# Linear attention feeding a sparse mixture of attention experts, on one core: key tails projected and multiplied once per two head pairs, part of the key sums by accumulating transfers, and the order of the steps as a list

## Chip, cores and metric

The kernel runs on one core of a Trainium2 chip. The metric is the device time of one execution in microseconds, 617.24 us as the median of three runs before the change (616.54 to 617.45).

## What is computed

The reference has two stages, each with B = 8 batches and S = 576 positions.

The first is linear attention over H = 8 heads of 64 columns. For q and k of every head a feature map phi projects 64 columns to 128, subtracts the largest absolute value of the row and takes exp of the result and of its negative, so that phi has 256 columns:

```python
proj = x @ w_phi; proj -= max(abs(proj), axis=-1)
phi = concatenate([exp(proj), exp(-proj)])
kv = phi(k).T @ v;  z = sum over positions of phi(k)
x = (phi(q) @ kv) / (phi(q) @ z + 1e-6)
```

The second takes x as [B, S, 512] and has E = 4 experts of causal softmax attention with a head of 64 columns each (projections wq, wk, wv, wo, scores scaled by 1/8). A gate of 4 logits per position picks the best two experts, and the output is their weighted sum.

## The kernel before

**Tiling.** Heads are taken in 32 pairs p (4 pairs for each batch b). 576 positions are 4 blocks of 128 and a tail of 64. The projections of phi, the products with v, z and the attention run in fp32; the three projections of x, the scores and the output projection run on a split of each operand into a high and a low part (hi, lo), as three matmuls hi x hi, hi x lo, lo x hi.

**Stages of a pair.** `load_k`, `load_q` and `load_v` bring the inputs on SP's queue. `stream_k` (L511) projects k: eight matmuls of 64 rows x 128 columns (`half_mm`, L506 to L509), one for each head and block, two of them side by side on the upper and lower 64 rows of the array, and a ninth for the tails of both heads. `center` (L558) takes the row maxima (L564) and subtracts them into `ek` (L578) on VectorE. ScalarE takes exp twice (act, L326, 1152 columns each). `key_sum` (L542) then adds the four blocks of phi(k) into `zs` by three VectorE additions (L546), for the pairs from p = 4 on. `stream_kv` (L589) multiplies: L605 has v's 32 columns as the weights and phi(k) as the moving operand, 4 blocks and a tail for each of two heads and two halves of v, 20 matmuls of 256 columns. L622 gives z: from p = 4 on with `zs` against ones and the tails against `sel`, 8 matmuls of 128 columns; before p = 4 with all five pieces, 20 matmuls. The result is turned (L641 or L633) and, from p = 6 on, sent through DRAM (`kvd`) into `kv`.

`stream_q` (L652) projects q, `phi_q` (L676) takes its maxima with GpSimd's PARTITION_ALL_REDUCE (L681), subtracts (L685) and takes exp. `stream_n` (L692) makes denominators (L710) and numerators (L721); `fractions` (L726) turns the denominators by VectorE (L732), adds eps by ScalarE into the PSUM bank, takes the reciprocal there (L739) and spreads it (L745); `divide` (L749) makes x in its hi and lo parts.

**Stages of a batch.** `stream_b` (L768) projects x to queries and keys (`proj_t`, L315 through the helper `mm`), makes scores (L838), copies them out (L324), masks them on GpSimd (L942). `maxima` (L945) finds the column maxima (L955, and PARTITION_ALL_REDUCE at L959), subtracts (L963) and starts the exps. `proj_v` (L859) projects x to values and gate logits: for each of 5 position blocks 12 matmuls of 260 columns, the fifth with 64 positions only. `sums` (L986, L1001), `attend` (L1010, L1030), `evac_y`, `out_unit` and `store` finish the batch.

**PSUM.** All products go through one pool of 8 banks of 512 columns, tag `c`. A bank is taken when a step is placed and given back at `plan.release`.

**Order.** Every engine works in the order in which the program's planner wrote the instructions (`in_order` fixes it). The planner is a list scheduler that runs while the program is built: each stream yields a `Step` with its engine and what it needs; `Plan.loop` picks, among the steps that could start within 53 ns of the earliest, the one with the lowest position (`MOVE`, `POS1`, `POS`, `BOFF`), with an allowance for a change of TensorE's tiling. Steps that copy out of PSUM choose between ScalarE and VectorE by cost. TensorE's tilings here are 128 x 128 (L315, L633), 64 rows x 128 columns (L509, L838) and 128 rows x 32 columns (L605, L622, L710, L721, L924, L1001, L1030).

```python
for t in range(NJ):
    for h in range(2):
        u_ = 4 * h + t if t < 4 else 8
        for k in range(2):
            g = slice(64 * k + 32 * h, 64 * k + 32 * h + 32)
            nc.tensor.matmul(o[g, 0:2], v_in[:, 4 * h + t if t < 4 else 8 + h, k:64:2], ...)
```

Of the kernel before, what the change touches and what calls it, by code (L numbers as in the profile page):

```python
# [26 lines left out]
KC = 640  # L27
# [9 lines left out]
CACT = ()  # L37
TAILPE = True
RB = 2
PXB = 5  # L40
HOT = 22.62
SLOPE = (-27.1, -45.11, 31.37, 22.04, 0.2)
UB = 4
SADD = 2
LAST = 7
KADD = 3
KPOOL = 0
FLEX = (544, -30)
QB = 1
PSUB = 0  # L50
# [4 lines left out]
WINDOW = 53.0  # L55
SWITCH = 43.0
SLACK = 150.0
LATE = (1200.0, 500.0)
PHASE = 0.0
ZEROS = 34.47  # L60

MOVE = {
# [32 lines left out]
NPAIRS = B * NP  # L95
HEAD = 2.29
ADDS = (0, 2)
KVD = 6
RATE = 2.18
TRATE = 2.37  # L100
CHANGE = (150.0, 190.0)
PORT = 350.0
OTHER = 20.47
LDW = 109.0
PSUM_TILES = (("c", 8, 512),)


def moved(x, i):
# [1048 lines left out]
```

## Time and profile before

| what | value |
|---|---|
| median of three runs | 617.24 us (616.54 to 617.45) |
| span of the profiled execution, first to last instruction | 615.0 us |
| time of the profiled execution by itself | not given apart from its span |
| instructions | 19992 |
| TensorE (PE) busy | 600.5 us, 98% |
| weight loads (PEld) busy | 470.6 us, 77% |
| VectorE (DVE) busy | 557.3 us, 91% |
| ScalarE (ACT) busy | 432.0 us, 70% |
| GpSimd (POOL) busy | 245.0 us, 40% |
| mean granted TensorE clock | 0.997 |
| moved by DMA | 52.48 MB |

A busy time is the union of an engine's instructions. Matmuls overlap: the next starts while the one before drains, so what a matmul costs the engine is the distance between starts, or the length of a piece of the chain of waits, and not its own duration. The chain of waits goes back from the last instruction to what released each one. A piece of it gives start, length, what ran and how often.

### The profile page before, as it was taken

What the parts mean: (1) busy time and instruction counts of PE and PEld (TensorE: products, weight loads), DVE (VectorE), ACT (ScalarE), POOL (GpSimd) and SP (SyncE); (2) the same over time, 40 slices, a digit from 0 to 9 for tenths busy, and PEclk for the clock granted to TensorE, in tenths of its full rate; (3) what the DMA queues carried; (4) which work ended last, traced back from release to release, by engine and by line L of the source; (5) the groups of instructions that cost most, each with busy time, mean ns of one, the idle gap of its engine ahead of it and who ended that gap; (6) DMA issues with size and microseconds to landing.
All of it is one profiled execution on the core that took longest, in us unless ns stands there. A gap on an engine that the chain in (4) does not pass through costs nothing.

```text
span 615.0 us, 19992 instructions
## 1 busy us (share of the span) xinstructions
PE 600.5 (98%) x8263; PEld 470.6 (77%) x8263; DVE 557.3 (91%) x1124; ACT 432.0 (70%) x1034; POOL 245.0 (40%) x167
## 2 busy tenths in 40 slices
PE   8999999999999999999999999999999999999987
PEld 7665788667796778768886868876889677878976
DVE  5899989999999999999899999999999998888793
ACT  4898786667687688677775885875796668556652
POOL 5635533453324644252333614418430706421420
PEclk9999999999999999999999999999999999999999
DMA  9553212253113431253214332144212311020022
GB/s 218 155 150 103 59 51 81 68 159 87 54 66 113 120 87 37 72 158 110 74 35 107 119 107 63 46 135 138 66 53 83 111 37 27 15 92 2 2 78 78
DMA packets 41610, 52.48 MB, mean 85 GB/s; under 512 B 21168, under 2 KB 24624, under 8 KB 41520
## 3 DMA queue, kind: packets, MB, share of 16 engines
q1 hardware_dynamic: 41200, 50.62, 28.5%
q8 instruction: 65, 1.06, 0.7%
q10 hardware_dynamic: 320, 0.59, 0.4%
q14 instruction: 25, 0.20, 0.1%
HBM read 36.64 MB, written 14.55 MB: 83 GB/s over the span
## 4 chain that ended last, share of the span: by engine, by line
PE 74%; DVE 15%; ACT 5%; DMA 2%; issue 2%; POOLq 1%; POOL 1%; SPq 0%; ACTq 0%; DVEq 0%
PE ps_c L315 29%; PE ps_c L509 9%; PE ps_c L605 9%; PE ps_c L721 7%; PE ps_c L1030 6%; PE ps_c L838 6%; PE ps_c L710 4%; DVE u L685 3%; DVE zs L546 2%; PE ps_c L622 2%; ACT ek L326 2%; PE ps_c L1001 1%; DVE s L963 1%; DVE ek L578 1%; DVE max L975 1%
## 5 line engine op out<-in xcount | busy, mean ns | idle before, releaser
L681 POOL PARTITION_ALL_REDUCE mx<-u x64 | 144.2, 2305 | 182.7 <-ACT u L324 165.9
L315 PE MATMUL ps_c<-xh,qk 128*128 128x320 f32 (+1 forms) x512 | 106.1, 298 | 0.0
L959 POOL PARTITION_ALL_REDUCE max<-top x16 | 59.9, 3745 | 101.5 <-DVE top L955 35.8
L315 PEld LDWEIGHTS ps_c<-xh,qk 128*128 128x128 f32 x512 | 82.7, 188 | 2.3 <-issue 0.7
L326 ACT ACTIVATE ek<-ek 128x1152 f32<-128x1152 f32 x64 | 75.0, 1171 | 5.7 <-DVE ek L578 5.0
L315 PE MATMUL ps_c<-xl,qk 128*128 128x256 f32 (+1 forms) x256 | 75.5, 295 | 0.0
L605 PE MATMUL ps_c<-ek,v_in 128*32 128x256 f32 x1280 | 75.4, 381 | 0.0
L963 DVE TENSOR_TENSOR s<-s,max 128x1152 f32<-128x1152 f32 (+4 forms) x80 | 68.3, 879 | 1.0 <-POOL max L959 1.0
L942 POOL TENSOR_SCALAR_AFFINE_SELECT s<-s 128x256 f32<-128x256 f32 (+1 forms) x80 | 41.5, 558 | 62.2 <-ACT s L324 61.9
L685 DVE TENSOR_TENSOR u<-u,mx 128x576 f32<-128x576 f32 x64 | 61.6, 975 | 3.9 <-POOL mx L681 3.9
L324 ACT COPY s<-ps_c 128x512 f32<-128x512 f32 (+4 forms) x152 | 52.7, 445 | 14.7 <-PE ps_c L838 14.4
L326 ACT ACTIVATE s<-s 128x1152 f32<-128x1152 f32 (+4 forms) x80 | 56.4, 740 | 8.6 <-DVE s L963 8.4
L605 PEld LDWEIGHTS ps_c<-ek,v_in 128*32 128x32 f32 x1280 | 39.7, 110 | 27.2 <-issue 1.3
L315 PE MATMUL ps_c<-vg,xh 128*128 128x260 f32 (+1 forms) x320 | 58.9, 286 | 0.3 <-ACT s L324 0.3
L564 DVE TENSOR_REDUCE pmax<-ps_c 128x4 f32<-128x512 f32 (+1 forms) x96 | 49.5, 539 | 8.1 <-PE ps_c L509 8.0
L315 PE MATMUL ps_c<-yh,wo 128*128 128x320 f32 (+1 forms) x256 | 53.1, 303 | 0.0
L326 ACT ACTIVATE mx<-u 128x576 f32<-128x576 f32 x64 | 43.9, 687 | 10.5 <-DVE u L685 10.4
L324 ACT COPY u<-ps_c 128x256 f32<-128x256 f32 (+1 forms) x127 | 41.6, 412 | 11.7 <-PE ps_c L509 11.4
L578 DVE TENSOR_TENSOR ek<-ps_c,pmax 128x512 f32<-128x512 f32 (+1 forms) x96 | 49.8, 537 | 0.0
L315 PEld LDWEIGHTS ps_c<-vg,xh 128*128 128x128 f32 (+1 forms) x320 | 47.4, 177 | 1.9 <-ACT s L324 0.8
L509 PEld LDWEIGHTS ps_c<-wf,k_in 64*128 64x128 f32 x576 | 41.9, 190 | 8.5 <-ACT u L324 3.0
L509 PE MATMUL ps_c<-wf,k_in 64*128 64x128 f32 x576 | 46.7, 283 | 1.5 <-ACT u L324 1.1
(124 smaller groups left out, 1399.4 us busy)
## 6 DMA issues: line engine op xcount, KB each, us to landing
v_in<-in_v_dram SPq DMA_DIRECT2D x32, 320.0 KB, 3.0
out_dram<-ot SPq DMA_DIRECT2D x32, 288.0 KB, 2.1
q_in<-in_qt_dram SPq DMA_DIRECT2D x60, 144.0 KB, 2.9
kvd<-kvt SPq DMA_DIRECT2D x104, 48.0 KB, 1.7
kv<-kvd SPq DMA_DIRECT2D x26, 192.0 KB, 2.6
k_in<-in_kt_dram SPq DMA_DIRECT2D x32, 144.0 KB, 2.8
k_in<-in_kt_dram SPq DMA_DIRECT2D x32, 128.0 KB, 2.8
q_in<-in_qt_dram ACTq DMA_DIRECT2D x4, 144.0 KB, 4.1
```

Source lines behind the costliest of these rows:

```text
L315: nc.tensor.matmul(o, a, b, start=start, stop=stop, skip_group_check=True)
L324: nc.scalar.copy(o, i)
L326: nc.scalar.activation(o, i, func, **kw)
L509: nc.tensor.matmul(o, a, b, start=True, stop=True, skip_group_check=True)
L564: dve(n * 128, [mk], [pk]).tensor_reduce(out=m[:, us], in_=src, axis=AX.X, op=ALU.max, apply_absolute_value=True)
L578: dve(n * 128, [e1k], [pk, mk]).tensor_tensor(out=ek2[p % EKB][:, 1, us, :], in0=src, in1=m[:, us].unsqueeze(2).to_broadcast([128, n, 128] ...
L605: nc.tensor.matmul(o[g, 0:2], v_in[:, 4 * h + t if t < 4 else 8 + h, k:64:2], ek[:, :, u_, :].rearrange("p c (w f) -> p c w f", w=4), star ...
L681: nc.gpsimd.partition_all_reduce(M, U, 128, bass_isa.ReduceOp.absmax)
L685: (nc.gpsimd if st.eng == 'POOL' else nc.vector).tensor_tensor(out=U, in0=U, in1=M, op=ALU.subtract)
L721: nc.tensor.matmul(ps[g:g + 32, 0:n], kvi[:, 2 * k + h, 32 * c:32 * c + 32], P_[h][c][:, s0:s1], start=c == 0, stop=c == 1, skip_group_che ...
L959: nc.gpsimd.partition_all_reduce(big.rearrange("p e s -> p (e s)"), top.rearrange("p e s -> p (e s)"), 128, bass_isa.ReduceOp.max)
L963: dve(2 * (S - 128 * j), [('d', x, j)], [('max', z)], 1.11, True).tensor_tensor(out=block(s_, j, None, rows(j)), in0=block(s_, j, None, ro ...
```

## The change

The parts of the diff, one by one. The first is the order: positions, costs and allowances of the planner go, and `Plan.loop` reads a list of 3100 characters, each the number of the stream that moves next. A second list of 520 digits says which engine makes each copy (0 ScalarE, 1 VectorE); 93 of the digits are 1. In the kernel before, VectorE made 32 such copies.

```diff
+    def loop(self):
+        sides = iter(SIDES)
+        for c in ORDER:
+            s = self.streams[ord(c) - 48]
...
+            if isinstance(st.eng, tuple):
+                st.eng = st.eng[int(next(sides))]
```

Key tails of four heads (two pairs) are loaded, projected, centred and put through exp together, as `kt_in`, `ekt`; k's main part keeps four blocks (`KC` 512, `ek` of 8 blocks, so exps of 1024 columns):

```diff
+    def load_tails():
+        for m in range(NT):
+            yield Step('SP', pred=has('proj_t', m - 1) if m else None)
+            src = kt[2 * m:2 * m + 2, :, 512:896].rearrange("q d (h t) -> (q d) h t", h=2)[:, :, 0:64]
+            load(kt_in.rearrange("p (h t) -> p h t", h=2), src, 'kt_in')
...
+    def stream_tails():
+        for m in range(NT):
+            banks = yield Step('PE', 'c', ready, n=2)
+            for a, (pk, ps) in enumerate(banks):
+                r = slice(64 * a, 64 * a + 64)
+                half_mm(ps[:, 0:128], kt_in[r, :], wf[r, 0:128], 128, pk, need)
...
+            act(256, ekt[:, 0], ekt[:, 1], ['et0'], ['et1'], AF.Exp)
+            yield Step('ACT')
+            act(256, ekt[:, 1], ekt[:, 1], ['et1'], [], AF.Exp, scale=-1.0)
```

Their products with v and with ones come first into the two PSUM banks of the two pairs, in a tiling of 64 rows x 32 columns, and the blocks are added to them. Both banks are taken before the first pair's products:

```diff
+    def tail_products(banks):
+        for h in range(2):
+            r = slice(64 * h, 64 * h + 64)
+            for k in range(2):
+                for a, (pk, ps) in enumerate(banks):
+                    g = 64 * k + 32 * (h ^ a)
+                    nc.tensor.matmul(three(ps)[g:g + 32, 0:2], vt_in[r, a, h, k:64:2], ekt[r, :, a].rearrange(...),
+                                     start=True, stop=False, skip_group_check=True)
...
+            if p % 2 == 0:
+                banks = yield Step('PE', 'c', lambda: ('phi_t', p // 2) in done and ('load_vt', p // 2) in done, n=2)
+                tail_products(banks)
+            odd, (kc, ps) = p % 2, banks[p % 2]
-            for t in range(NJ):
+            for t in range(4):
...
-            for t in range(first + TAILPE if adds else NJ):
+            for t in range(1 if adds else 4):
```

The sum of the blocks of phi(k): blocks 0 and 1 are written to `zs` by ScalarE as exps of their own (two of 512 columns), blocks 2 and 3 are added to them by one transfer with accumulation from GpSimd's queue, and VectorE adds the two halves:

```diff
+        if adds:
+            yield Step('ACT', pred=has('kv', p - 1))
+            for c in range(2):
+                act(512, zs[:, c].rearrange("p a h f -> p (a h) f"), ek[:, 1, 0:4], ['zs'], [e1k], AF.Exp, scale=1.0 - 2.0 * c)
...
+    def key_sum(p, ek, ekk):
+        yield Step('POOL')
+        add_to(zs.rearrange("p c a h f -> p c (a h f)"), ek[:, :, 4:8, :].rearrange("p c u f -> p c (u f)"), 'zs', ekk)
+        yield Step('DVE')
+        dve(512, ['zs'], [], 1.11, True).tensor_tensor(out=zs[:, :, 0], in0=zs[:, :, 0], in1=zs[:, :, 1], op=ALU.add)
...
+    def add_to(o, i, w, r):
+        nc.gpsimd.dma_start(o, i, accum_op=ALU.add)
```

The factors of `fractions` lie in SBUF (`facs`, two buffers for each of its two uses), so the PSUM bank goes back after the first turn:

```diff
-        both = ps[:, S // 2:S // 2 + 18]
+        both, fk = facs[a][n % 2], f'fac{a}{n % 2}'
         dve(S // 2, [key], [pk], 1.15).transpose(X[:, 0:S // 2], ps[:, 0:S // 2])
+        plan.release('c', (pk, ps))
...
-        plan.release('c', (pk, ps))
```

In `proj_v` the fifth block takes the last 64 positions of x's hi and lo parts side by side as 128 weight columns (`x_end`, copied by ScalarE after `divide`), 8 matmuls where there were 12; the lower half of the result is copied out by ScalarE and the upper half added to it by VectorE:

```diff
+        if s1 == S:
+            yield Step('ACT')
+            act(128, x_end[i], xT2[i][:, :, S - 64:S], [f'xe{i}'], [f'xh{i}', f'xl{i}'])
...
+                    for x_, w_ in ((0, 0), (0, 1), (1, 0)) if m == 128 else ((None, 0), (None, 1)):
...
+                act(260, vs[:m, j], ps[m:128, 0:260], [f'vs{j}', 'lg'], [kc])
+                yield Step('DVE')
+                dve(260, [f'vs{j}', 'lg'], [kc]).tensor_tensor(out=vs[:m, j], in0=ps[:m, 0:260], in1=vs[:m, j], op=ALU.add)
```

The loads follow: k in two transfers a pair for three, v with 8 blocks for 10, and for every two pairs one transfer of key tails and one of v's tails.

## Rows read from the trace of the kernel before

**Rows 1.** Page, busy time by engine, and the chain of waits by engine.

```profile
PE 600.5 (98%) x8263; PEld 470.6 (77%) x8263; DVE 557.3 (91%) x1124; ACT 432.0 (70%) x1034; POOL 245.0 (40%) x167
PE 74%; DVE 15%; ACT 5%; DMA 2%; issue 2%; POOLq 1%; POOL 1%; SPq 0%; ACTq 0%; DVEq 0%
```

**Rows 2.** Busy time by stretch: stretch, length, PE, PEld, DVE, ACT, POOL (instructions), clock, DMA.

```profile
0.00:25.00 25.00, 22.85 (x299) 18.46 (x299) 16.93 (x47) 15.25 (x29) 13.01 (x13) 1.00 0.78 199
...
250.00:275.00 25.00, 25.00 (x400) 17.06 (x400) 23.49 (x54) 16.10 (x46) 12.61 (x5) 1.00 0.44 131
...
575.00:600.00 25.00, 22.37 (x304) 20.21 (x300) 22.10 (x42) 16.95 (x43) 8.32 (x7) 0.98 0.13 49
600.00:615.00 15.00, 11.06 (x124) 9.21 (x116) 4.56 (x10) 3.78 (x12) 0.00 (x0) 0.92 0.21 80
```

**Rows 3.** Chain of waits in order of time: start, length, work (xcount).

```profile
14.40 1.31 PE ps_c L509 x18
...
257.34 1.09 PE ps_c L509 x16
...
260.73 0.44 PE ps_c L622 x16
...
268.84 2.30 PE ps_c L605 x40
...
293.27 2.16 PE ps_c L605 x40
...
298.62 0.89 PE ps_c L509 x16
```

**Rows 4.** Timeline of PE, the fifth block of the value projection: start, length, work.

```profile
584.41 0.40 PE L315 MATMUL ps_c<-vg,xh 128*64 128x260 f32 x2
...
585.85 0.40 PE L315 MATMUL ps_c<-yh,wo 128*128 128x256 f32 x2
```

**Rows 5.** Groups by line and form, PE's warm-up matmuls.

```profile
L315 PE MATMUL ps_c<-warm 128*128 128x128 bf16 x117 | 8.8, 241 | 1.0 <-DVE col L356 1.0
```

**Rows 6.** Groups by line and form, VectorE: busy us, mean ns.

```profile
L546 DVE TENSOR_TENSOR zs<-zs,ek 128x512 f32<-128x512 f32 x56 | 42.4, 757 | 0.5
L546 DVE TENSOR_TENSOR zs<-ek 128x512 f32<-128x512 f32 x28 | 21.6, 772 | 0.6 <-ACT ek L326 0.4 <-PE ps_c L622 0.2
L1044 DVE TENSOR_TENSOR ps_c<-ps_c,rb 128x256 f32<-128x256 f32 x16 | 6.7, 418 | 0.4 <-PE ps_c L1030 0.2
```

**Rows 7.** Groups by line and form, ScalarE: busy us, mean ns.

```profile
L326 ACT ACTIVATE ek<-ek 128x1152 f32<-128x1152 f32 x64 | 75.0, 1171 | 5.7 <-DVE ek L578 5.0
L326 ACT ACTIVATE s<-s 128x640 f32<-128x640 f32 x16 | 11.8, 739 | 0.8 <-DVE s L963 0.8
L326 ACT ACTIVATE s<-s 128x384 f32<-128x384 f32 x16 | 8.4, 526 | 0.0
L326 ACT ACTIVATE s<-s 64x128 f32<-64x128 f32 x16 | 4.8, 302 | 0.3 <-DVE s L963 0.3
L324 ACT COPY u<-ps_c 128x256 f32<-128x256 f32 x64 | 20.7, 377 | 10.8 <-PE ps_c L509 10.5
```

**Rows 8.** The tile of key sums: count, shortest/median/longest ns, first and last start.

```profile
L622 PE MATMUL ps_c<-zs,ones x224: 272/273/298, 53.9 to 522.5; 128*32 128x128 f32 x112
```

**Rows 9.** DMA issues: queue, count, KB each, us to landing.

```profile
v_in<-in_v_dram SPq DMA_DIRECT2D x32, 320.0 KB, 3.0
...
kvd<-kvt SPq DMA_DIRECT2D x104, 48.0 KB, 1.7
kv<-kvd SPq DMA_DIRECT2D x26, 192.0 KB, 2.6
```

**Rows 10.** Timeline, VectorE beside GpSimd, at the start of the kernel.

```profile
8.10 8.50 POOL L681 PARTITION_ALL_REDUCE mx<-u  x4 [6.79 <-ACT u L324]
...
11.53 0.74 DVE L685 TENSOR_TENSOR u<-u,mx 128x576 f32<-128x576 f32 x1
...
12.40 1.86 DVE L685 TENSOR_TENSOR u<-u,mx 128x576 f32<-128x576 f32 x1
```

**Rows 11.** Waits of PE: waiter, what ended it, us in total, times, longest.

```profile
PE ps_c L1001 <- DVE max L975: 2.6, 1, 2.6
...
PE ps_c L509 <- ACT u L324: 1.1, 2, 0.6
```

More of the change, by code (lines that the diff above doesn't have):

```diff
@@ L181, in run @@
             cost = self.clocked(t, cost, rows)
-        if port:
+        if eng == 'DVE' and port:
             cost += self.blocked(t)
+            self.shared = (t, t + cost)
+        if eng == 'POOL' and self.shared[0] < t < self.shared[1]:
+            t = self.shared[1]
         end = t + cost
@@ L186, in run @@
         if eng == 'POOL':
-            self.pool = [*self.pool[-7:], (t, end)]
+            self.pool = [*self.pool[-7:], (t, t + port)]
         for k in r:
@@ L231, in release @@
         self.psum[tag].append(t)
-    def start(self, st):
-        best = None
-        for eng, cost in st.eng if isinstance(st.eng, tuple) else ((st.eng, 0.0),):
-            t = self.free.get(eng, 0.0)
-            for k in st.needs:
-                t = max(t, self.after(self.ready, k, eng) + st.slack)
-            if st.tag is not None:
-                t = max(t, sorted(self.after(self.last, k, eng) for k, _ in self.psum[st.tag])[st.n - 1])
-            if eng == 'DVE' and st.port:
-                cost += self.blocked(t)
-            if best is None or t + cost < best[0]:
-                best = t + cost, t, eng
-        return best[1:]
@@ L273, in loop @@
                 self.streams.remove(s)
+        assert not self.streams
 def in_order(tc):
@@ new lines, in stream_k, with phi_k @@
+            done.add(('proj_k', p))
+            plan.spawn(phi_k(p))
+    def phi_k(p):
+        i = p % EKB
+        ek, e0k, e1k = ek2[i], f'ek{i}0', f'ek{i}1'
+        adds = ADDS[p >= NP]
+        yield Step('ACT', pred=lambda: all((('center', p, t) in done for t in range(2))))
+        act(1024, ek[:, 0], ek[:, 1], [e0k], [e1k], AF.Exp)
+        if adds:
[3 more added lines that the diff above has]
+        yield Step('ACT')
+        act(1024, ek[:, 1], ek[:, 1], [e1k], [], AF.Exp, scale=-1.0)
+        if adds:
+            plan.spawn(key_sum(p, ek, [e0k, e1k]))
+        done.add(('phi_k', p))
@@ new lines, in stream_tails @@
+    def stream_tails():
+        for m in range(NT):
+            need = ['kt_in', 'wphi']
+            ready = lambda: ('load_t', m) in done and ('w', 0) in done and (not m or ('kvt', m - 1) in done)
+            banks = yield Step('PE', 'c', ready, n=2)
+            for a, (pk, ps) in enumerate(banks):
+                r = slice(64 * a, 64 * a + 64)
+                half_mm(ps[:, 0:128], kt_in[r, :], wf[r, 0:128], 128, pk, need)
+            done.add(('proj_t', m))
+            for a, (pk, ps) in enumerate(banks):
+                plan.spawn(center_tail(m, a, pk, ps))
+            yield Step('ACT', pred=lambda: all((('center_t', m, a) in done for a in range(2))))
+            act(256, ekt[:, 0], ekt[:, 1], ['et0'], ['et1'], AF.Exp)
+            yield Step('ACT')
+            act(256, ekt[:, 1], ekt[:, 1], ['et1'], [], AF.Exp, scale=-1.0)
+            done.add(('phi_t', m))
@@ L559, in center @@
         m, mk = pmax[p % 2], ('pmax', p % 2, t)
-        us = slice(4 * t, min(9, 4 * t + 4))
-        n = us.stop - us.start
-        src = ps[:, 0:n * 128].rearrange("p (u f) -> p u f", f=128)
-        yield Step('DVE', [pk], hot=True)
-        dve(n * 128, [mk], [pk]).tensor_reduce(out=m[:, us], in_=src, axis=AX.X, op=ALU.max,
-                                               apply_absolute_value=True)
-        free = has('kv', p - EKB) if p >= EKB else None
-        e0k, e1k = f'ek{p % EKB}0', f'ek{p % EKB}1'
@@ L568, in center @@
[L568 to L579 removed]
+        us = slice(4 * t, 4 * t + 4)
@@ L589, in stream_kv, with three @@
+    def three(ps):
+        return ps[:, 0:384].rearrange("p (w c f) -> p c w f", w=4, c=3)
     def stream_kv():
+        banks = None
         for p in range(NPAIRS):
@@ L895, in gates @@
         G = 'gate'
-        yield Step('DVE', ['lg'], pred=lambda: all(('v', b, j) in done for j in range(NJ)) and (not b or ('gate', b - 1) in done))
+        yield Step('DVE', pred=lambda: all((('v', b, j) in done for j in range(NJ))) and (not b or ('gate', b - 1) in done))
         dve(80, [G], ['lg'], port=True).tensor_tensor(out=ge, in0=lg.unsqueeze(3).to_broadcast(sh4),
@@ L938, in mask @@
         sk = [('S', x, IN_BANK[j][0], e) for e in range(2)]
-        yield Step('POOL', sk, pred=lambda: all(('S', n, IN_BANK[j][0], e) in done for e in range(2)))
-        plan.run('POOL', 260 + 1.3 * 2 * w, [('m', x, j)], sk)
+        yield Step('POOL', pred=lambda: all((('S', n, IN_BANK[j][0], e) in done for e in range(2))))
+        plan.run('POOL', 230 + 0.65 * 2 * w, [('m', x, j)], sk, port=100 + 1.3 * w)
         d = ss[x][:w, :, KEYS[j]:KEYS[j] + w]
```

541 lines of the change are left out of this document (254 added, 287 removed), and 16 rows, old and new, of the table MOVE.

## Prediction, made before the changed kernel ran

> **What bounds the kernel now.** I read the page's busy times first, then the busy times by stretch, then the chain of waits, and last the waits of PE. PE is busy for 600.5 of 615.0 us, DVE for 91%, ACT for 70%, and the chain that ended last is 74% PE and 15% DVE [rows 1]. A busy PE may still be waiting inside the pipeline, so the stretches decide: of PE's 14.5 us without work, 2.15 lie in the first 25 us and 2.63 + 3.94 in the last 40, which leaves 5.8 us for the 550 between [rows 2]; there whole stretches are full. In such a stretch the chain is a string of PE pieces end to end [rows 3], and PE's own waits are single events, 2.6 us and 0.6 us at most [rows 11]. So PE sets the time nearly everywhere, and the question is what the change takes from its queue. DVE is next, near enough that it would take over if PE lost more than some 40 us.
>
> The span of the one profiled execution is 615.0 us; its own time isn't given, and the median of the runs is 617.2, so 2.2 us lie around the span. I carry every difference over to 617.2. About 0.2% (1.2 us) is what a measurement of this kernel can tell from no change.
>
> **PE, removed.** The 40 instructions of one pair's kv products take 2.16 us [rows 3], 0.054 each; two instructions are one fp32 matmul. The tail is 8 of the 40: 0.43 us a pair, 13.8 us for 32 pairs. In z, 16 instructions take 0.44 us [rows 3], and the tails are 8: 0.22 us, 7.0 for 32 (the four early pairs, with 20 matmuls, also lose one fifth of theirs, the same 8 instructions). The projection of k takes 1.31 us with the ninth matmul and 1.09 without [rows 3]: 0.22, again 7.0. The fifth block of the value projection takes 12 matmuls from 584.41 to 585.85 [rows 4], 0.12 each; four go in each of 8 batches: 3.8 us. Together 31.6 us.
>
> **PE, added.** For each of 16 groups of four heads: two projections side by side. A lone ninth matmul takes 0.22 us, and the eight that run two by two take 0.89 [rows 3], so a couple takes 0.22 as well and the second half is free: 16 x 0.22 = 3.5 us. Then 8 tail products of 256 columns and 8 of 128 for z, in tiles of 64 rows x 32 columns. No row has this tiling. The rows bound it: four column tiles side by side take 0.43 and 0.22 us, and the two row halves ran side by side in the projection. If all eight overlap, a group costs 0.65 us, 10.4 in all; if the halves take turns, 1.30, 20.8 in all. I take 10.4, since the projection's overlap is the nearest row, and keep the other end as a rival. Added: 13.9 us. So PE's work falls by 17.7 us.
>
> **Changes of tiling.** The kv products take 2.30 us after work in another tiling and 2.16 after work in their own; the projection of k 1.09 and 0.89 [rows 3]. A change thus costs 0.14 to 0.20 us, say 0.17. The tails' projection can stand beside another one of 64 x 128 at no change, or alone at two; the tail products add one or two. Between 1 and 4 a group, that is 2.7 to 10.9 us; I take one and a half, 4.1, because the projections are frequent and the blocks' products can follow the tails'.
>
> **What is covered.** In the start PE is short of work: 117 warm-up matmuls fill 8.8 us there [rows 5]. The first four pairs' savings (one eighth of 13.9 = 17.7 - 3.8) only make room for more of these, 1.7 us. In the last 35 us the chain goes through GpSimd, DVE and ACT, and PE's value projection of the last batch lies under it: 0.5 us. So 2.2 us of the gain are lost.
>
> **VectorE.** 84 additions take 64.0 us [rows 6]; 56 go, 42.7 us. Eight additions in the fifth value block come, 0.42 each [rows 6], 3.3. The list gives DVE 93 copies instead of 32: 61 at 0.42 to 0.45, some 26. DVE falls by about 13 to 544 us, still 90% of a 602 us kernel. None of this is on the path while PE is full; if PE is not the bound, this 13 us is what remains, so that case ends at the same time and needs no price of its own.
>
> **ScalarE.** Between 384 columns (0.526) and 640 (0.739) [rows 7] an exp of 512 takes 0.63: 56 of them, 35 us. The 64 exps of phi(k) shrink by 128 columns (0.11 each by the same slope), -7. Tail exps of 256 columns, between 0.302 for 128 and 0.526 for 384, 0.41: 32, 13 us. `x_end`, 32 at 0.30, 10. The 61 copies that leave take 0.38 or more [rows 7]: -23 or -24. ACT rises by 27 to about 459 us, 76%: hidden, as ACT's idle time is 30% now. The two new exps stand ahead of the second exp of phi(k), so the kv products of a pair come 1.3 us later; DVE's additions are gone after that, and phi(k) has two buffers.
>
> **Factors in SBUF and PSUM banks.** The copies with eps and the reciprocal stay as many. A bank comes back before them and not after. Against that, the two kv banks are now held from the first pair's tail products to the second pair's copy, up to two pair periods. The trace shows no price: a wait for a bank is at most 0.6 us in the rows [rows 11], so 16 groups give at most 16 x 0.6 = 10 us of loss, and the earlier release may give back the few us of waits. I take it as nothing, by the smallness of the waits.
>
> **The accumulating transfer.** It moves 512 KB for each of 28 pairs. No row has a transfer from GpSimd's queue or one with addition. At the rate of v's load (320 KB in 3.0 us) it would land in 4.8 us, at that of `kv` (192 KB in 2.6) in 6.9, at that of `kvd` (48 KB in 1.7) in 18.1 [rows 9]. I take 7, since its rows are long like those of the first two. It issues on GpSimd's queue, 40% busy [rows 1], and waits there for the second exp; what stands behind it (maxima of q, masks, maxima of scores) waits along, which costs nothing while the queue is idle 370 us. How much time has it? The first z matmul starts at 53.9 and the last at 522.5 [rows 8], 28 pairs, 17.4 us each. `zs` is one buffer: in each period come two exps (1.26), the exp of phi(k) (1.06), the transfer, one addition (0.76) and z (0.22), 3.3 us and the transfer. So it may take 14.1 us before it limits the pairs. SP's queue issues the same number of transfers as before (one less a pair, two more for two pairs).
>
> **The order.** That the order is a list, and which list, the profile cannot price. At best it closes PE's idle time in the middle, 5.8 us, most of that in the last 40, 6.6, and some changes of tiling; at worst it opens as much. I take 4 us of gain: DVE's additions for z, which PE waited behind, are fewer, and the choice of copying engine is more even.
>
> **Sum.** 617.2 - 31.6 + 13.9 + 4.1 + 2.2 - 4.0 = 601.8; I forecast 602 us.
>
> **Rivals.**
> *A. The tail tiles take turns.* Both row halves of a tail product write the same two banks, while in every projection and score of the kernel before the upper and lower half have a bank each, so no row shows halves meeting in a bank. If they take turns, 10.4 us come back: 612. For it speaks that nothing in the trace excludes it, against it that four column tiles write one bank side by side in every kv product [rows 3]. The Trainium skill's TensorEngine Tiling (Array Packing), Restrictions and Gotchas, says that different row tiles cannot access the same PSUM bank at the same time; by that rule A is what happens, and no run here shows it yet.
> *B. The order does more.* If the list also closes the idle time in the middle and at the end (another 8 us) and saves as many changes as the tails add (4), the time is 590. For it: changes are short but many; against it: PE is full in the middle already.
> *C. The transfer is late: slower.* Place: the wait of z for `zs` in PE's queue, with the products of the next pairs, q's projection and the batch's projections behind it. Point: 14.1 us from issue to landing. Each us beyond is paid 27 times: at 14.7 us the gain of 15 is gone, at 15.5 the time is 602 + 1.4 x 27 = 640. For it: 18.1 us by the slowest row, and GpSimd's queue, on which PARTITION_ALL_REDUCEs of 2 us each stand. Contention with DVE is visible: of two subtractions in one run of them, one takes 0.74 us and the next 1.86 [rows 10]. Against it: both long-row transfers are far below the point. The Trainium skill's SBUF — State Buffer, on the "DVE blocks DMA" trap, says that GpSimd cannot write a transfer's descriptors while DVE holds the port that they share; this speaks against the change, and no trace here has such a transfer.
> *D. The kv banks starve PE.* With the 10 us above and no gain from the order, 602 + 4 + 10 = 616: no change.
>
> **Chances.** Forecast 0.45 (594 to 609); A 0.20 (608 to 616); B 0.15 (580 to 594); C 0.12; D 0.08, evenly around 616. Faster by over 0.2% (below 616.0): 0.45 + 0.19 + 0.15 + 0.03 = 0.82; I say 0.79, since the order's own loss (the worse end of its term) has no case here. Within 0.2%: 0.06. Slower: 0.15, C with half of what is left of D. The range 588 to 617 leaves out C and the lower third of B, some 2 in 10. It holds the ends of the tiles' cost (612) and of the changes (608.6).
>
> **What would show it.** Right: L605's successor has 32 instructions a pair in 1.73 us; a group's tail products last 0.65 us; PE's share stays at 97% or more; zs additions number 28; the transfers land in 5 to 8 us. A shows as tail products of 1.3 us a group. C shows as waits of PE for DVE's addition to `zs`, 28 times, with landings above 14 us. D shows as PE waiting for copies of `kvt` or for banks. The forecast is wrong if PE's busy time falls by less than 8 us, or if it falls by 13 and idle time takes its place.

## The result, and the profile after

The changed kernel takes 607.68 us (median of four runs, 607.37 to 607.85) against 617.35 of the kernel before, run beside it (616.54 to 617.63): a ratio of 0.9856, 95% interval 0.984 to 0.9873. The medians lie 9.7 us apart and the interval says 7.8 to 9.9, where 15.4 were forecast. The span of the profiled execution is 605.8 us, at a granted clock of 0.999; before it was 615.0. So 9.2 us of span went, and these are what has to be explained.

The page of the changed kernel, busy time by engine and the chain of waits by engine (to be held against [rows 1]):

```profile
PE 582.0 (96%) x7909; PEld 447.9 (74%) x7909; DVE 553.5 (91%) x1172; ACT 449.2 (74%) x1087; POOL 275.1 (45%) x195
...
PE 63%; DVE 18%; DMA 7%; ACT 5%; issue 4%; POOL 2%; SPq 1%; DVEq 0%; POOLq 0%; ACTq 0%
```

PE's busy time fell by 18.5 us (600.5 to 582.0), but the span fell by 9.2 only: PE now has 23.8 us without work (605.8 - 582.0), where it had 14.5. In the chain PE's share went from 74% to 63%, and DMA's from 2% to 7%. So PE was relieved of work, and idle time took half of its place. Where it did, the busy time by stretch shows (columns as in [rows 2]), first of the changed kernel and below it of the kernel before:

```profile
50.00:200.00 150.00, 142.58 (x1938) 106.48 (x1931) 140.64 (x282) 116.49 (x284) 74.50 (x53) 1.00 0.48 112
200.00:350.00 150.00, 147.12 (x2029) 112.49 (x2025) 138.21 (x302) 116.57 (x283) 72.27 (x51) 1.00 0.51 121
350.00:500.00 150.00, 146.25 (x1962) 114.19 (x1954) 141.40 (x292) 111.85 (x276) 66.39 (x48) 1.00 0.46 114
```

```profile
50.00:200.00 150.00, 147.82 (x2013) 112.71 (x2011) 142.55 (x283) 110.07 (x257) 63.80 (x42) 1.00 0.29 83
200.00:350.00 150.00, 148.74 (x2044) 117.32 (x2042) 142.93 (x283) 107.59 (x266) 66.09 (x44) 1.00 0.33 94
350.00:500.00 150.00, 149.10 (x2109) 116.40 (x2108) 141.37 (x288) 106.48 (x256) 58.63 (x39) 1.00 0.29 86
```

PE's idle time in these three is 7.4 + 2.9 + 3.8 = 14.1 us, where the kernel before has 2.18 + 1.26 + 0.90 = 4.3. So the new idle time lies in the middle, and this is the stretch in which the new transfers run.

The chain of waits of the changed kernel between 50 and 150 us (start, length, work), eight pieces of it:

```profile
43.00 8.98 DMA zs<-ek
...
52.00 0.70 DVE zs L560
...
52.75 0.42 PE ps_c L621 x8
...
58.15 1.73 PE ps_c L610 x32
...
72.50 0.59 PE ps_c L577 x16
73.09 0.22 PE ps_c L585 x16
73.31 1.87 PE ps_c L610 x32
75.17 0.22 PE ps_c L621 x8
```

The last five pieces are the joined tails at work. L610 is the successor of L605: 32 instructions in 1.73 us, 1.87 after the tails' tiling. A group's tail products take 0.59 + 0.22 us. z (L621) takes 0.22. The first three pieces are a transfer on the chain: it is issued at 43.00 and lands 8.98 us later, the addition comes at 52.00, and z only then.

Groups by line and form (busy us, mean ns, idle before):

```profile
L318 POOL DMA_DIRECT2D zs<-ek x28 | 34.2, 1223 | 94.4 <-ACT ek L292 65.7 <-PE ps_c L485 9.9 <-ACT u L290 7.8
...
L292 ACT ACTIVATE zs<-ek 128x512 f32<-128x512 f32 x56 | 32.2, 625 | 7.8 <-PE ps_c L621 7.5
...
L560 DVE TENSOR_TENSOR zs<-zs 128x512 f32<-128x512 f32 x28 | 21.4, 764 | 9.2 <-DMA zs<-ek 9.1
...
L621 PE MATMUL ps_c<-zs,ones 128*32 128x128 f32 x224 | 11.5, 276 | 5.8 <-DVE zs L560 5.6
...
L281 PE MATMUL ps_c<-warm 128*128 128x128 bf16 x51 | 5.3, 264 | 1.1 <-DVE col L325 1.1
```

VectorE stands 9.1 us for landings ahead of the addition, in 6 of the 28 pairs, and PE 5.6 us for the addition ahead of z, in 4. GpSimd takes 1.22 us for each issue and stands 65.7 us in its own queue until ScalarE's second exp lets it issue. The DMA issues of the page (queue, count, KB, us to landing):

```profile
zs<-ek POOLq DMA_DIRECT2D x28, 512.0 KB, 6.2
...
q_in<-in_qt_dram SPq DMA_DIRECT2D x60, 144.0 KB, 4.1
k_in<-in_kt_dram SPq DMA_DIRECT2D x64, 128.0 KB, 3.7
```

The transfers land in 6.2 us (median). In the three stretches above the DMA engines are busy for 0.46 to 0.51 of their time (last column but one).

**A part of the diff that the text ahead of the prediction left out.** The constant `SADD` went from 2 to 4. With it the row sums of the attention are formed by four VectorE additions instead of two for each of the 16 head pairs of the attention (8 batches, 2 pairs), and PE multiplies two blocks with ones for each where it had four. It is 32 additions more on VectorE and 256 short matmuls fewer on PE. The prediction has no term for it; an experiment below gives its price.

### The profile page after: what moved, and what is told of

Same layout as the page of the kernel before. It is cut to its first block, busy times and chain, and to the rows that moved or that the text cites. A ratio compares the mean times of both kernels' runs of the same rounds, so it can differ in the third digit from the quotient of the medians.

```text
span 605.8 us, 19534 instructions
## 1 busy us (share of the span) xinstructions
PE 582.0 (96%) x7909; PEld 447.9 (74%) x7909; DVE 553.5 (91%) x1172; ACT 449.2 (74%) x1087; POOL 275.1 (45%) x195
## 4 chain that ended last, share of the span: by engine, by line
PE 63%; DVE 18%; DMA 7%; ACT 5%; issue 4%; POOL 2%; SPq 1%; DVEq 0%; POOLq 0%; ACTq 0%
PE ps_c L281 26%; PE ps_c L485 7%; PE ps_c L718 6%; PE ps_c L838 6%; PE ps_c L610 5%; PE ps_c L1034 5%; DMA zs<-ek 5%; PE ps_c L707 4%; DVE s L967 3%; DVE top L959 2%; ACT ek L292 1%; PE ps_c L621 1%; DVE u L682 1%; DMA q_in<-in_qt_dram 1%; DVE max L979 1%
## 5 line engine op out<-in xcount | busy, mean ns | idle before, releaser
L680 POOL PARTITION_ALL_REDUCE mx<-u x64 | 146.0, 2319 | 45.2 <-ACT u L290 22.9
L281 PE MATMUL ps_c<-x,qk 128*128 128x256 f32 (+1 forms) x768 | 106.6, 298 | 0.0
L281 PEld LDWEIGHTS ps_c<-x,qk 128*128 128x128 f32 x768 | 102.4, 189 | 4.4 <-ACT u L290 1.0
L318 POOL DMA_DIRECT2D zs<-ek x28 | 34.2, 1223 | 94.4 <-ACT ek L292 65.7
L967 DVE TENSOR_TENSOR s<-s,max 128x1152 f32<-128x1152 f32 (+4 forms) x80 | 73.2, 944 | 0.0
L292 ACT ACTIVATE ek<-ek 128x1024 f32<-128x1024 f32 x64 | 67.7, 1058 | 3.6 <-DVE ek L551 2.8
L610 PE MATMUL ps_c<-ek,v_in 128*32 128x256 f32 x1024 | 61.7, 381 | 0.5 <-ACT ek L292 0.5
L281 PE MATMUL ps_c<-yh,wo 128*128 128x256 f32 (+1 forms) x256 | 52.7, 300 | 0.0
L290 ACT COPY u<-ps_c 128x320 f32<-128x320 f32 (+1 forms) x107 | 40.1, 402 | 12.7 <-PE ps_c L485 11.9
L281 PE MATMUL ps_c<-vg,x 128*128 128x260 f32 x384 | 49.1, 285 | 0.0
L1034 PE MATMUL ps_c<-s,vs 128*32 128x320 f32 (+4 forms) x896 | 46.5, 357 | 2.0 <-DVE ql L791 2.0
L281 PEld LDWEIGHTS ps_c<-vg,x 128*128 128x128 f32 x384 | 47.1, 188 | 0.8 <-issue 0.2
L610 PEld LDWEIGHTS ps_c<-ek,v_in 128*32 128x32 f32 x1024 | 31.4, 110 | 21.8 <-issue 2.7
L548 DVE TENSOR_REDUCE pmax<-ps_c 128x4 f32<-128x512 f32 x64 | 42.7, 680 | 2.7 <-PE ps_c L485 2.5
L485 PE MATMUL ps_c<-q_in,wf 64*128 64x256 f32 (+1 forms) x256 | 43.5, 442 | 1.1 <-DVE ek L551 1.0
```

Source lines behind the costliest of these rows:

```text
L281: nc.tensor.matmul(o, a, b, start=start, stop=stop, skip_group_check=True)
L290: nc.scalar.copy(o, i)
L292: nc.scalar.activation(o, i, func, **kw)
L485: nc.tensor.matmul(o, a, b, start=True, stop=True, skip_group_check=True)
L548: dve(512, [mk], [pk]).tensor_reduce(out=m[:, us], in_=src, axis=AX.X, op=ALU.max, apply_absolute_value=True)
L610: nc.tensor.matmul(o[g, 0:2], v_in[:, 4 * h + t, k:64:2], ek[:, :, 2 * TURN[t] + h, :].rearrange("p c (w f) -> p c w f", w=4), start=False ...
```

## The experiments

The kernel before was run again beside each of them (medians 616.5 to 616.8), so times are compared by their ratio to it. One thousandth is 0.62 us, and an interval is 1 to 2 us wide to either side; the changed kernel stands at 0.9856. The line numbers shift by a few from kernel to kernel. All but the last two are made from the changed kernel, with every step at its place in the list unless the text says otherwise.

**The additions back on VectorE.** Left out are the exps into `zs` and the transfers.

```diff
-        add_to(zs..., ek[:, :, 4:8, :]..., 'zs', ekk)
-        ...tensor_tensor(out=zs[:, :, 0], in0=zs[:, :, 0], in1=zs[:, :, 1], op=ALU.add)
+        ...tensor_tensor(out=zs[:, :, 0], in0=ek[:, :, 0:2], in1=ek[:, :, 2:4], op=ALU.add)
+        ...tensor_tensor(out=zs[:, :, 0], in0=zs[:, :, 0], in1=ek[:, :, 4:6], op=ALU.add)
+        ...tensor_tensor(out=zs[:, :, 0], in0=zs[:, :, 0], in1=ek[:, :, 6:8], op=ALU.add)
```

> The changed kernel took 607.7 us. Here the accumulating transfer and the two exps into zs are undone: VectorE makes all three additions of a pair, in the same places of the listed order. TensorE's waits for the sum go, VectorE gets 43 us more and stands near 600 us of work. Theory Q (TensorE's queue sets the time, and what is lost against the forecast are its waits for the sum of keys): VectorE becomes the bound, 612 to 625. Theory V (VectorE, 91% busy, already sets the time): the whole 43 us show, 635 to 650. Theory L (the transfer itself is the loss, the additions were hidden): 598 to 604.

Measured: 632.2 us, ratio 1.0251 (1.0235 to 1.0267), slower than the kernel before. Its page:

```profile
PE 596.4 (95%) x7909; PEld 451.6 (72%) x7909; DVE 592.6 (94%) x1228; ACT 420.5 (67%) x1031; POOL 248.8 (39%) x167
...
DVE 43%; PE 40%; issue 8%; ACT 4%; POOL 3%; DMA 1%; DVEq 0%; SPq 0%; ACTq 0%; POOLq 0%
```

The time lies between the range for PE's queue and the one for VectorE, 3 us below the latter. VectorE leads the chain with 43%. In this list 39 us more on VectorE (592.6 against 553.5) cost 24 us, though ScalarE lost 29 us and the transfers were gone. PE, too, is busy 14.4 us longer with the same 7909 instructions, at a mean granted clock of 0.984 where the changed kernel had 0.999; how much of the 24 us goes with that, no run shows. Without moving the additions off VectorE, this list is slower than the kernel before.

**z without its wait.** z of the pairs from the fifth on reads a constant; the sum is still made (left out: its use).

```diff
-    nc.tensor.matmul(o[g:g + 32, 2], ones, x_..., ...)
+    nc.tensor.matmul(o[g:g + 32, 2], big if adds else ones, ones.unsqueeze(1).to_broadcast([128, 4, 32]) if adds else x_..., ...)
```

> The sums z of the pairs from the fifth on leave out the sum of the key blocks: the same four matmuls read a constant in its place, so TensorE doesn't wait for the transfer and the addition, which are still made. Theory Q: 9 to 10 us go, 598 to 601. Theory V: VectorE's work is the same, 606 to 608. Theory L (the transfer disturbs through its traffic, not through the wait): 605 to 608.

Measured: 604.9 us, ratio 0.9823 (0.9803 to 0.9843). About 2 us are gained, against 5.6 us that PE's matmuls of z wait in the trace of the changed kernel. Its page:

```profile
PE 584.9 (97%) x7909; PEld 450.8 (75%) x7909; DVE 551.5 (91%) x1173; ACT 447.7 (74%) x1087; POOL 275.5 (46%) x195
```

PE's idle time did fall by the 5.6 us (from 23.8 to 603.1 - 584.9 = 18.2), but its busy time rose by 2.9 with the same instructions, at a mean granted clock of 0.992 against 0.999, and ate half of that. The 9 to 10 us that theory Q held didn't come; the time lies 0.1 us below theory L's 605 to 608 (the traffic disturbs, and not the wait). So PE's wait for the sum is worth about 2 us and isn't where most of the missing time is.

**The row sums back on PE.** `SADD` 2 again in effect, the steps at their places.

```diff
+            if j <= 2:
+                eng.tensor_tensor(...)
...
+        pieces = [(block 0), (maxs[n % MB][:, :, 128:S], 64, True, False)] + [(block(s_, j), 64 * j, False, j == NJ - 1) for j in range(3, NJ)]
```

> The row sums of the attention are made with two additions on VectorE and the last two blocks on TensorE, as before the change (a part of the diff that the prediction did not price). TensorE gets 256 small matmuls, 5.8 us, VectorE loses 32 additions, 14 us. Theory Q: 611 to 614. Theory V: 594 to 600. If both bind in turn: 606 to 610.

Measured: 610.4 us, ratio 0.9889 (0.9869 to 0.9909), 2 us slower, at the edge of what the intervals tell. That lies between the 606 to 610 expected if both engines bind in turn and the 611 to 614 if only PE counted, and far from the 594 to 600 if only VectorE did. VectorE's busy time is 543.2 us here and 553.5 with the change, PE's 584.2 and 582.0. So the overlooked part moved 10.3 us onto VectorE and 2.2 off PE, and is worth about 2 us.

**The fifth value block as before.** 12 matmuls of 64 weight columns, no copies into `x_end` and no addition of the halves.

```diff
-            act(128, x_end[i], xT2[i][:, :, S - 64:S], ...)
...
-                dve(260, ...).tensor_tensor(out=vs[:m, j], in0=ps[:m, 0:260], in1=vs[:m, j], op=ALU.add)
+                        nc.tensor.matmul(ps[:m, 0:260], xs[c][x_][:, 512:576], wvg[w_]..., start=n == 0, stop=n == 11)
```

> The fifth block of the value projection with 12 matmuls of 64 positions as before, without the copies of the ends of x and without the addition of the two halves. TensorE gets 3.8 us, ScalarE loses 9, VectorE 3. Theory Q: 610 to 612. Theory V: 604 to 606.

Measured: 609.0 us, ratio 0.9879 (0.9856 to 0.9901): 1.4 us slower, but the intervals overlap, and it lies in neither of the expected ranges (610 to 612, 604 to 606). The forecast had 3.8 us for it on PE; PE's busy time rose by 2.2 (584.2) and VectorE's fell by 3.2 (550.3).

**Less work on one engine, on the other, on both.** These three ask which engine a microsecond counts on.

```diff
-        ....tensor_reduce(out=m[:, us], in_=src, axis=AX.X, op=ALU.max, ...)
+        ....tensor_reduce(out=m[:, us], in_=src[:, :, 0:80], axis=AX.X, op=ALU.max, ...)
```

> The changed kernel with VectorE's row maxima of phi(k) read over 80 of the 128 columns of each head (this is left out of the computation: 48 columns of every maximum), 64 instructions shorter by about 0.23 us each, some 15 us less on VectorE; nothing moved, every wait as it was. The changed kernel takes 607.7 us. Theory P (PE's queue alone sets the time): 605.7 to 608. Theory V (VectorE sets it, PE's waits come from VectorE being full): 592 to 596. Theory B (both are nearly full and wait for each other in turn): 599 to 605.

```diff
                     for w_, x_ in ((0, 0), (0, 1), (1, 0)):
+                        if x_ and c in (1, 2):
+                            n += 1
+                            continue
                         mm(ps[:, 0:s1 - s0], w[w_][:, o:o + 128], xs[c][x_][:, s0:s1], ...)
```

> The changed kernel without 2 of the 12 matmuls of each of the 64 accumulations of x's projections to queries and keys (left out: two of the four low-by-high terms), 128 matmuls of 256 or 320 columns at about 0.12 us, some 15 us less on PE; nothing moved, every wait as it was. The changed kernel takes 607.7 us. Theory P (PE alone): 591 to 595. Theory V (VectorE): 605.5 to 608. Theory B (both in turn): 597 to 605.

> Both cuts at once: VectorE's row maxima over 80 of 128 columns and two of twelve matmuls fewer in each projection of x (both left out of the computation), some 15 us less on VectorE and 15 us less on PE. Theory P: as with PE's cut alone, 590 to 595. Theory V: as with VectorE's cut alone, 590 to 596. Theory B: 589 to 595 while each cut alone stays above 597, so that the two together give clearly more than either.

Measured: less on VectorE 605.3 us, ratio 0.9819 (0.9801 to 0.9836); less on PE 603.9, 0.9791 (0.9776 to 0.9806); both 601.2, 0.9754 (0.9719 to 0.9788). Busy time by engine of the second and, below it, of the third:

```profile
PE 568.2 (94%) x7781; PEld 431.0 (72%) x7781; DVE 553.3 (92%) x1172; ACT 448.9 (75%) x1087; POOL 278.0 (46%) x195
```

```profile
PE 569.6 (95%) x7781; PEld 432.5 (72%) x7781; DVE 543.6 (91%) x1172; ACT 448.3 (75%) x1087; POOL 282.0 (47%) x195
...
PE 52%; DVE 19%; DMA 12%; ACT 7%; issue 5%; POOL 3%; SPq 2%; DVEq 0%; POOLq 0%; ACTq 0%
```

PE lost 13.8 us of work for 4.0 us of time, VectorE 10.4 for 2.3 (553.5 to 543.1), and both together 22 to 24 for 6.3. All three theories fall: P and V by the single cuts, and B, which 603.9 fits and 605.3 misses by 0.3 us, because both cuts together give no more than the sum of the single gains and stay far above 589 to 595. What holds the time is not the work of these two engines alone. In the chain of the last kernel DMA has risen to 12%.

**z later in the list.** The attempt at a better version: z stands up to two PE steps later.

```diff
+            if held and (held[0] is s or held[1] <= 0 or not (st.pred is None or st.pred())):
+                self.advance(held[0], None)
+                held = None
...
+            if hasattr(st, 'late'):
+                held = [s, 2]
+                continue
```

> The changed kernel with one thing moved: from the fifth pair on, the z products of a pair stand up to two PE steps later in the list (earlier only where the next step needs them). PE's waits for the sum in zs were 14.4 us in 22 events; taking the wait away outright gave 2.8 us. Theory Q (the list puts z too early, the wait can be filled): 603 to 606, with waits of PE for zs under 5 us. Theory B (the wait is replaced by the next one on DVE's results, and each move out of its place can add a change of tiling of 0.14 to 0.20 us on either side): 607 to 612, with waits for zs shorter but PE no faster.

Measured: 613.7 us, ratio 0.9942 (0.9919 to 0.9965), 5 us slower than the changed kernel. The waits of PE's matmuls for `zs` fell from 5.6 to 2.0 us, as wanted (the 14.4 us in the expectation are these 5.6 and the 8.8 of the weight loads, which stand over the same time, in 12 events together), but PE's busy time is 586.5 us against 582.0: z now stands between work in other tilings, and what waits for z comes later. Which of the two weighs more was not tried. This one move did not better the list.

**No transfer.** The issue is taken out; the exps into `zs`, VectorE's addition and the waits for it stay. Left out are blocks 2 and 3 of the key sums.

```diff
-        nc.gpsimd.dma_start(o, i, accum_op=ALU.add)
```

> The changed kernel without the 28 accumulating transfers (left out of the computation: blocks 2 and 3 of the key sums). The exps into zs, VectorE's one addition and the wait of z for it stay, so z waits only for ScalarE and VectorE, GpSimd's queue loses 28 issues of 1.22 us and the DMA engines 14.7 MB. The changed kernel takes 607.7 us; with z freed of every wait for zs, but the transfer running, it took 604.9. Theory T (the transfer costs more than its wait: it crowds the loads, holds GpSimd's queue ahead of the maxima of q, and delays VectorE): 598 to 603. Theory L (the transfer lies beside other work, and the wait is all it costs): 603.5 to 606.5.

Measured: 595.2 us, ratio 0.9656 (0.9643 to 0.9669). Neither theory held so much: 12.3 us come from 28 transfers (11 to 14 by the two intervals). Its page and its three stretches:

```profile
PE 581.7 (98%) x7909; PEld 449.2 (75%) x7909; DVE 551.7 (93%) x1172; ACT 449.1 (75%) x1087; POOL 243.3 (41%) x167
...
PE 75%; DVE 16%; issue 3%; DMA 2%; ACT 2%; POOL 1%; SPq 1%; DVEq 0%; ACTq 0%; POOLq 0%
```

```profile
50.00:200.00 150.00, 148.68 (x2027) 111.63 (x2020) 143.12 (x295) 123.28 (x297) 67.22 (x45) 1.00 0.29 81
200.00:350.00 150.00, 149.04 (x2039) 115.09 (x2038) 142.09 (x302) 115.72 (x282) 66.97 (x43) 1.00 0.34 95
350.00:500.00 150.00, 148.09 (x2034) 115.37 (x2033) 142.89 (x297) 116.58 (x284) 60.82 (x42) 1.00 0.30 87
```

The busy times of PE, VectorE and ScalarE are the changed kernel's within 2 us. The DMA engines are busy for 0.29 to 0.34 of the three stretches instead of 0.46 to 0.51. What is gone is idle time: PE has 14.1 us of it (595.8 - 581.7), as the kernel before had 14.5, and 4.2 instead of 14.1 in the three stretches, where the kernel before has 4.3. So in this list all the idle time that took the place of the saved work hangs on the transfer. (The profiled execution took 598.0 us, 2.8 more than the median, so these idle times are rather too high than too low.) Two more traces of the transfer are seen here. The loads land sooner without it (count, KB, us to landing):

```profile
q_in<-in_qt_dram SPq DMA_DIRECT2D x60, 144.0 KB, 3.0
k_in<-in_kt_dram SPq DMA_DIRECT2D x64, 128.0 KB, 2.9
```

and GpSimd is ahead of its input for the maxima of q (waits of GpSimd: us in total, times, longest; below it the changed kernel, where GpSimd also stands 65.7 us for the exp that releases a transfer):

```profile
POOL mx L679 <- ACT u L290: 63.6, 15, 11.9
```

```profile
POOL mx L680 <- ACT u L290: 22.9, 9, 3.7
```

GpSimd's idle time ahead of the maxima went from 63.6 us to 22.9 with the transfer: more often the input is already there when GpSimd comes to it. But hardly anyone is seen to wait for these later maxima. VectorE's subtraction of them, in the changed kernel, has 0.2 us of idle time before all 64 of its instructions together:

```profile
L682 DVE TENSOR_TENSOR u<-u,mx 128x576 f32<-128x576 f32 x64 | 51.6, 816 | 0.2 <-POOL mx L680 0.2
```

It is 0.2 us without the transfer as well, and before the subtractions of the scores' maxima (L967) it is 0.0 in the changed kernel. In the chain GpSimd has 2% with the transfer and 1% without.

**The transfer sent aside.** Same source, size and place in the queue, but it adds into `aside`, a tile of 128 x 1024 in DRAM that nobody reads (left out: blocks 2 and 3 of the key sums).

```diff
-        add_to(zs..., ek[:, :, 4:8, :]..., 'zs', ekk)
+        nc.gpsimd.dma_start(aside..., ek[:, :, 4:8, :]..., accum_op=ALU.add)
```

> The changed kernel with the 28 accumulating transfers sent aside: same source, same size, same place in GpSimd's queue, but they add into a buffer in DRAM that nobody reads (left out of the computation: blocks 2 and 3 of the key sums; the first of the 28 writes without adding). So nobody waits for a landing, neither VectorE's addition nor z, while the issues, their wait in GpSimd's queue and the traffic stay. With the transfer the kernel takes 607.7 us, without it 595.2, so 12.5 us are to be divided. Theory W (the waits for the landing are the cost, on PE and above all on VectorE with all that stands behind its addition): 595 to 598.5. Theory K (the cost is the traffic and GpSimd's queue, which make loads and maxima late): 603 to 608. Between: 598.5 to 603.

Measured: 602.6 us, ratio 0.9764 (0.9744 to 0.9784), between the theories. Its page, and its transfer:

```profile
PE 582.2 (97%) x7909; PEld 449.1 (75%) x7909; DVE 556.1 (92%) x1172; ACT 449.6 (75%) x1087; POOL 270.4 (45%) x195
...
PE 69%; DVE 20%; issue 3%; DMA 3%; ACT 2%; POOL 1%; SPq 1%; DVEq 0%; POOLq 0%; ACTq 0%
```

```profile
aside<-ek POOLq DMA_DIRECT2D x28, 512.0 KB, 5.9
...
q_in<-in_qt_dram SPq DMA_DIRECT2D x60, 144.0 KB, 4.0
k_in<-in_kt_dram SPq DMA_DIRECT2D x64, 128.0 KB, 3.8
```

Of the 12.3 us, 5.7 are the waits for the landing (0.9856 - 0.9764), and 6.6 the presence of the transfer alone, each to within some 1.5 us by the intervals: the loads stay as slow as in the changed kernel (4.0 and 3.8 us), and GpSimd's queue is as full. The division has two weaknesses: the destination lies in DRAM, though the landing is nearly the same, and the next writer of phi(k)'s buffer still waits until the transfer has read it. How the 6.6 us divide between the loads, GpSimd's queue and this buffer isn't settled; no kernel kept one without the others. VectorE's 0.2 us of waits for the maxima speak against the queue. For the loads speaks that the profile has a late landing of q on the chain of waits, here of the changed kernel and below it of this one:

```profile
278.24 7.44 DMA q_in<-in_qt_dram
```

```profile
275.31 6.68 DMA q_in<-in_qt_dram
```

Between 50 and 550 us of the kernel without the transfer, the longest landing on the chain is 3.9 us.

**The same cuts in the kernel before,** in its own order, by the edits shown above:

> The kernel before, in its own order, without 2 of the 12 matmuls of each projection of x to queries and keys (the same 128 matmuls as in the cut of the changed kernel, left out of the computation), some 14 us less on PE. In the changed kernel this cut gave 3.7 us. Theory P0 (the kernel before was bound by PE, as its windows were read): 602 to 606, a gain of 11 to 14. Theory B0 (VectorE bound it in turn already, and the windows hid it): 609 to 614, a gain of 3 to 8.

> The kernel before, in its own order, with VectorE's row maxima of phi(k) read over 80 of the 128 columns in the 64 instructions of four blocks (48 columns of every maximum left out), 10 us less on VectorE by the same cut of the changed kernel, where it gave 2.5 us. Theory P0 (PE bound it): 615.5 to 617.5, no change. Theory B0: 611 to 615.

Measured: less on PE 611.2 us, ratio 0.9917 (0.9903 to 0.993); less on VectorE 614.6, 0.9971 (0.9959 to 0.9982). The page of the first:

```profile
PE 588.8 (97%) x8135; PEld 455.8 (75%) x8135; DVE 560.0 (92%) x1124; ACT 430.0 (71%) x1034; POOL 247.5 (41%) x167
...
PE 44%; DVE 32%; ACT 16%; issue 4%; DMA 2%; POOL 1%; POOLq 1%; SPq 0%; DVEq 0%; ACTq 0%
```

and the chain of the second:

```profile
PE 86%; DVE 9%; ACT 2%; issue 1%; DMA 1%; POOLq 1%; SPq 0%; POOL 0%; DVEq 0%
```

11.7 us less on PE gave 5.1 us of time, 11.0 less on VectorE (557.3 to 546.3) gave 1.8. P0 falls for both: also the kernel before, with PE busy for 98%, was not bound by PE alone. After the cut on PE its share of the chain is 44%, and VectorE and ScalarE hold 48%; after the cut on VectorE PE holds 86%. Each cut moves the chain towards the engines that were not cut, as when they bind in turn.

## Why the prediction was right in direction and short by a third

**Right, with their sizes.** *The kv products:* 32 instructions in 1.73 us, as the sum had it. *z:* 0.22 us where nothing is waited for. *The tail tiles overlap:* a group of tail products takes 0.59 + 0.22 = 0.81 us; with one change of tiling of the forecast's 0.17 taken off it is 0.64, against 0.65 by full overlap and 1.30 by turns. Rival A is refuted. The Trainium skill's TensorEngine Tiling (Array Packing), Restrictions and Gotchas, has different row tiles unable to access one PSUM bank at the same time; these products do share their banks, and the trace shows no turns. *The changes of tiling:* 1.87 - 1.73 = 0.14 us for the products behind the tails. *VectorE:* 544 us forecast, 543.2 measured with the row sums put back as they were. *The transfer's landing:* 7 us taken, 6.2 measured; 28 additions; the exps into `zs` 0.625 us, forecast 0.63. Rival C's point of 14.1 us wasn't reached (the longest landing is 9.0 us in the profile of the tile), and D does not show: PE's two waits for copies of `kvt` that the trace has are 0.4 us each, and its longest wait that can be one for a bank, behind VectorE's `ql` (L791), is 2.0 us, once.

**Wrong: the step "The accumulating transfer".** The prediction took it to be free below its limit of 14.1 us per pair: "what stands behind it ... waits along, which costs nothing while the queue is idle 370 us". The runs show 12.3 us in its place: 5.7 us of waits for landings and 6.6 us from its presence. The landing was sized rightly and the period rightly; the conclusion was not. A limit per period says when a resource is saturated. It doesn't say that a chain of two exps, issue, 6 us of landing, addition and z fits between its neighbours in three queues that are each worked off in a fixed order. Of the two costs the prediction had looked for, the queue's is the one that doesn't show: GpSimd's queue stood 65.7 us behind the transfer's wait for an exp, with maxima behind it, but VectorE waited 0.2 us for those. The slower loads, the other candidate for the 6.6 us, it had no term for. The Trainium skill's SBUF — State Buffer, SBUF: two separate sides, on the "DVE blocks DMA" trap, has GpSimd unable to write descriptors while VectorE runs an operation that holds their shared port. The trace shows no such delay at the issue: the 28 took 1.20 to 1.37 us each beside a VectorE that was busy for 91%; how many of VectorE's operations are of that kind it doesn't say. What it shows is VectorE slowed beside GpSimd, in the timeline around 413 us:

```profile
412.61 3.59 POOL L963 PARTITION_ALL_REDUCE max<-top  x1 [4.51 <-DVE top L959]
...
413.27 2.00 DVE L560 TENSOR_TENSOR zs<-zs 128x512 f32<-128x512 f32 x1 [0.85 <-DMA zs<-ek]
```

and in the profile of the tile, for all 28 issues and additions (shortest, median, longest ns):

```profile
L318 POOL DMA_DIRECT2D zs<-ek x28: 1202/1218/1369, 43.0 to 513.4; - x28
L560 DVE TENSOR_TENSOR zs<-zs x28: 622/684/1998, 52.0 to 523.8; 128x512 f32<-128x512 f32 x28
...
DMA to landing us min/median/max: 5.0/6.2/9.0
```

This addition, released by a landing, began 0.66 us after a PARTITION_ALL_REDUCE and took 2.00 us instead of 0.68, with z behind it. Two others that began as soon after one took 1.26 and 1.17; the rest, of which nine also fell beside one, took 0.62 to 0.84. This is not where the 12.3 us are: the mean of the 28 is 764 ns, 80 above the median, 2.2 us in all, and in the kernel before it was 757 and 772 [rows 6].

**Wrong: "The order", -4.0 us.** Idle time did not close; it opened by 9.3 us. Without the transfer it is back where it was (14.1 against 14.5), so the gain that the list was to bring doesn't show there either. What the list does by itself is not shown: no run has it without the other parts, or these without it.

**Too small: PE's work.** Forecast was -17.7 + 4.1 = -13.6 us, with 1.7 us more warm-up filling in the start; PE's busy time fell by 18.5. The warm-up matmuls went from 117 to 51 and from 8.8 to 5.3 us [rows 5], 5.2 us below the forecast, and the overlooked row sums are 2.2 us. These two account for the difference, within a microsecond.

**The sum again, from spans.** Forecast were -11.9 us of busy time (-13.6 + 1.7) and -3.5 of idle time (-4.0 + 0.5), together -15.4. Measured are -18.5 and +9.3, together -9.2. Two misses of opposite sign, 6.6 us of busy time and 12.8 of idle time, left 6.2 us between them, so the total is nearer than its terms. That is luck: the extra busy time saved is warm-up work and a part of the diff that the prediction had not priced. By the prediction's own signs the mechanism held only in part: PE's share was to stay at 97% or more and is 96%, and the forecast was to be wrong if PE's busy time fell by 13 us and idle time took its place; idle time took half of the 18.5. The range, 588 to 617 us, is wide enough to hold the result all the same.

**The reading "PE sets the time nearly everywhere" was too strong.** It stood on full windows and on PE's short waits [rows 2, 11]. Both are true, and yet a microsecond off PE was worth 0.44 us in the kernel before (5.1 of 11.7) and 0.29 in the changed one (4.0 of 13.8). VectorE was at 91% and its chains lay only a little behind. In the changed kernel they are the chain itself for whole stretches: between 121.8 and 146.3 us it has no piece of PE. Some pieces of it, from the same view as above:

```profile
125.07 2.12 DVE top L959
...
133.03 4.41 DVE s L967 x2
...
146.31 0.79 PE ps_c L1005 x16
```

Here the maxima and subtractions of the scores run, and PE fills in around them. Without the transfer 18.8 us off PE went with 19.2 us off the span, a microsecond for each, but in that kernel VectorE's additions were gone too (632.2 us with them) and the list was another. How much of it the order of the kernel before would have given, no run shows. Nor are 0.44 and 0.29 prices for any place: the row sums put back on PE took 10.3 us off VectorE and put 2.2 on PE, which by the prices of the cuts (2.3 of 10.4 and 4.0 of 13.8) is a gain of 1.6 us, and the kernel was 2 us slower.

## What to carry to other kernels

A full engine in a window doesn't price a cut on it: take the same microseconds out of it in a kernel that leaves work out, and see what they are worth. Cost a transfer that replaces arithmetic at two places at least, the wait of its reader (5.7 us here) and what its presence does to the loads and queues beside it (6.6 us here, not divided further); its landing time against the period prices neither. Before blaming a queue that stands, look whether anyone waits for what is behind it. And read a diff of constants as closely as one of functions: one constant here moved 10 us from one engine to the other.

## What was not expected of the hardware

- Products of the upper and the lower 64 rows of the array accumulated into the same two PSUM banks side by side (in each bank the two halves write different column tiles): 16 instructions of 256 columns in 0.59 us and 16 of 128 columns in 0.22, the latter no more than 8 of them take in a tiling of four column tiles.
- 14.7 MB of accumulating transfers, in 28 pieces that landed in 6.2 us (median), made the loads of q and k land 1.1 and 0.8 us later (3.0 to 4.1 and 2.9 to 3.7 us), although the DMA engines were busy for only half of the time. A transfer with addition into DRAM did the same.
- z after a wait for VectorE is a piece of 0.42 us in the chain, without one 0.22. That is not twice the cost: in the timeline the next group starts 0.24 us after z, while z's last matmuls are still on their way:

```profile
52.75 0.42 PE L621 MATMUL ps_c<-zs,ones 128*32 128x128 f32 x8 [2.27 <-DVE zs L560]
52.99 0.67 PE L707 MATMUL ps_c<-mx,kv 128*32 128x288 f32 x8
```
